# Score tile, exponentials and order of the value matmuls in a chunked-attention and routed-FFN kernel

## The chip, the cores and the metric

The kernel runs on one core of a Trainium2 chip. The metric is the device time of one execution in microseconds. A core has a matrix engine (TensorE, PE in the profile; its weight loads are the row PEld), a vector engine (VectorE, DVE), an activation engine (ScalarE, ACT), GpSimd (POOL), which here issues most DMAs, and a sync engine (SyncE, SP), which issues the others. PE writes to PSUM, eight banks of 128 partitions x 512 fp32.

## The reference

There are two steps. The first is attention over chunks, with 4 batches of 8 heads, 768 positions and 64 channels. Each chunk of 32 queries sees 8 memory keys and a window of the sequence around it:

```python
for c in range(nc):                       # chunk 32, left 16, right 8
    l_start, r_end = max(0, c * 32 - 16), min(S, c * 32 + 32 + 8)
    k_full = np.concatenate([mem_k, k[:, :, l_start:r_end]], axis=2)
    v_full = np.concatenate([mem_v, v[:, :, l_start:r_end]], axis=2)
    scores = np.matmul(q_c, k_full.transpose(0, 1, 3, 2)) / np.sqrt(D)
    a = softmax(scores)
    out[:, :, c * 32:c * 32 + 32] = np.matmul(a, v_full)
```

The second takes the result as x (4 batches, 768 rows, 512 columns). Per batch it scores each row by `x @ w_gate`, chooses the 128 highest, and adds `sigmoid(score) * relu(xe @ w1) @ w2` to those rows (w1 is 512 x 1024, w2 is 1024 x 512).

## The kernel before, in words

The unit of the attention is a pair of heads; there are 16 pairs (n = 0 to 15), four to a batch. The order on every engine is the order of the program text, written out by hand.

For each pair the stages are these. `tr_q` (L213) transposes q by 16 PE matmuls into PSUM, and ACT copies the result to `qT` (L219). `tr_k` (L227) does the same for k; DVE lays it out as overlapping windows in `kw` (L232), and POOL writes the memory keys into the gaps (L224). `tr_v` (L237) does v, with ACT's copy to `vw` (L242), and `back_v` (L245) transposes the windows back, with DVE's copy to `vc` (L251). `scores(n, half)` (L256) makes 8 matmuls into a PSUM tile of two banks, and ACT makes three exponentials of it (L271), one per mask column, each of 256 elements a partition. `values(n, half)` (L277) makes 12 matmuls into one bank: six of 96 output partitions and six of 32, which go to partitions 96 to 127. In the text all of the 96s come first, then all of the 32s (L288 to L293). DVE takes the reciprocal of the sums (L295) and writes x (L296). The transposes have 64 output columns of the array, the scores 64 rows, `back_v` the whole array.

PSUM is full: four banks for two score tiles (pool `pss`), one for the values (`pxx`), one for q's and `back_v`'s transposes (`pvv`), one for k's and v's (`ptt`), one for the second step (`pmm`).

The loop (L539 to L575) works on three pairs at once. In pass n it makes the first half of the scores of pair n+1, `tr_q(n+2)`, the first half of the values of pair n, `tr_k(n+2)`, the second half of the scores of n+1, `back_v(n+1)`, the second half of the values of n, and `tr_v(n+2)`. Between the stages stand eight hooks; hook 8n+j holds steps of the second step of the batch before, by a table of places (L477 to L483). `fill` matmuls of zeros (L114) stand where PE would do little.

The second step for a batch is: dots of x with w_gate on DVE (`m_dot`, L335), the scores as a row (`m_row`), comparisons of all with all on DVE (`m_cmp`, L373), counts by PE (`m_count`, L383), mask, slot and a one-hot matrix `sel` on DVE (`m_slot`, L398; `m_sel`, L405), the row numbers by PE and DVE (`m_aux`, L438 and L441), the fetch of the rows from DRAM by an indirect DMA of POOL (`m_fetch`, L412), their transposes (`m_rows`, L419), two FFN stages with ACT between them (L453, L455, L462, L465), and an indirect DMA that adds y to the output (L466). Batch 2 has its slot, sel and fetch at place 24, which is the start of pair 15; its FFN stands in the tail (L578 to L602). Batch 3 is done in the tail. It works in the banks of the score tiles and gathers its rows by PE from an f16 copy of x (`m_x16`, L340) instead of a DMA.

Weights and inputs come by POOL's DMAs, and SP stores x for batches 0 to 2 (L319, L320), POOL for batch 3.

Of the kernel before, what the change touches and what calls it, by code (L numbers as in the profile page):

```python
# [8 lines left out]
FP = mybir.dt.float32  # L9
# [17 lines left out]
def kernel(  # L27
# [13 lines left out]
    nc = tc.nc  # L41
# [72 lines left out]
    def fill_into(ap, n=1):  # L114
        for _ in range(n):
            nc.tensor.matmul(out=ap, lhsT=zeros[:, 0:128], rhs=zeros, start=True, stop=True)  # L116
# [138 lines left out]

    def scores(n, half, fills=0):  # L256
        if n >= NPR:
            return
        kw, qT = kws[n % SLOTS], qTs[n]
        qf = qT.rearrange("p t j -> p (t j)")  # L260
        p_s = pss.tile([128, 2, 512], FP, tag="ps", name="p_s")
        fill_into(p_s[:, 0, :], fills)
        for gi, g in enumerate(GROUPS[half]):
            for h in range(2):
                o = 64 * h
                nc.tensor.matmul(out=p_s[:, h, 96 * gi:96 * gi + 96], lhsT=kw[o:o + 64, g, :],  # L266
                                 rhs=qf[o:o + 64, 96 * g:96 * g + 96], start=True, stop=True)
        es = att.tile([128, 2, 4, 96], F16, tag="es", name="es")
        pv = p_s[:, :, 0:384].rearrange("p s (g t) -> p s g t", t=96)
        for c in range(3):  # L270
            nc.scalar.activation(out=es[:, :, :, 32 * c:32 * c + 32], in_=pv[:, :, :, 32 * c:32 * c + 32],  # L271
                                 func=AF.Exp, bias=maskb[:, c:c + 1], scale=0.125)
        ess[n, half] = es

    xs = {}

    def values(n, half, fills=0):  # L277
        b, pr = divmod(n, NP)
        if pr == 0 and half == 0:
            xs[b] = xpool.tile([128, NB, Dm], FP, tag="x", name=f"x{b}")  # L280
        es, vc = ess.pop((n, half)), vcs[n % SLOTS]
        if n == NPR - 1:
            p_w = pss.tile([128, 2, 512], FP, tag="ps", name="p_w")[:, 0, :]
        else:
            p_w = pxx.tile([128, 512], FP, tag="px", name="p_w")
        fill_into(p_w, fills)
        p_x = p_w[:, 0:390].rearrange("p (i h c) -> p i h c", i=3, h=2)
        for r0, r1, gis in ((0, 96, (0, 1, 2)), (96, 128, (3, 3, 3))):  # L288
            for i, gi in enumerate(gis):
                q0, q1 = (0, 96) if gi < 3 else (32 * i, 32 * i + 32)  # L290
                for h in range(2):
                    nc.tensor.matmul(out=p_x[r0:r1, i, h, :], lhsT=es[:, h, gi, q0:q1],  # L292
                                     rhs=vc[:, GROUPS[half][gi], h, 0:65], start=True, stop=True)  # L293
        rd = att.tile([128, 3, 2, 1], FP, tag="rd", name="rd")
        nc.vector.reciprocal(out=rd, in_=p_x[:, :, :, 64:65])  # L295
        nc.vector.tensor_tensor(  # L296
            out=xs[b].rearrange("p g (n h d) -> p n g h d", n=NP, d=D)[:, pr, 3 * half:3 * half + 3],
            in0=p_x[:, :, :, 0:64], in1=rd.to_broadcast([128, 3, 2, D]), op=ALU.mult)
# [7 lines left out]
    LAST = B - 1  # L306

    def m_bank(b, shape, dt=FP):

        if b == LAST:  # L310
            t = pss.tile([128, 2, 512], FP, tag="ps", name="p_l")
            return t
        return pmm.tile([128, 1, 512], FP, tag="pm", name="p_m")
# [155 lines left out]
    def moe_steps(b):  # L469
# [53 lines left out]
    fill(3)  # L523
    scores(0, 0)
    mem_rows(memv16, memvT)
# [4 lines left out]
    tr_k(1)  # L530
    scores(0, 1)
    fill(2)
# [3 lines left out]
    late_constants()  # L536
    scrA = mod.tile([128, NB], FP, tag="scrA", name="scrA")
    scrB = mod.tile([128, NB], FP, tag="scrB", name="scrB")
    for n in range(NPR):  # L539
# [98 lines left out]
```

## Time and profile before

| what | value |
|---|---|
| median of 3 runs | 139.21 us (139.1 to 145.28) |
| the profiled execution | 139.08 us, span of its profile 137.4 us |
| busy: PE, PEld | 111.7 us (81%), 83.0 us (60%) |
| busy: DVE, ACT, POOL | 87.5 us (64%), 80.0 us (58%), 50.5 us (37%) |
| mean granted PE clock | 0.936 of full |
| values matmuls L292 | 384, busy 24.4 us |
| exponentials L271 | 96, mean 485 ns, busy 38.8 us |
| end of the loop (last x of pair 15) | 111.9 us into the span |

The chain that ended last is spread over the engines: PE 31%, DVE 15%, ACT 14%, issue 14%, DMA 14%, POOL 6%. The granted clock was half of full from 61.7 to 68.5 us, from 106 to 112.8 us and at the very end. In the timeline a line gives the start and the length in us, the engine, the source line, the operation with its tiles, `128*96` for the rows and columns of the array that a matmul uses, and in brackets how long the engine stood idle before it and what ended that. A run of equal instructions is one line with its count; matmuls are pipelined, so the length of such a line goes past the start of the next.

### The profile page before, as it was taken

The numbers are of one execution on the slowest core, as the hardware profiler recorded it, in microseconds if no ns is written. First come the engines' busy times: TensorE is split into PE (matmuls) and PEld (weight loads), VectorE is DVE, ScalarE is ACT, GpSimd is POOL, SyncE is SP. The second block draws the span as 40 slices with busy tenths as digits, with TensorE's granted clock in tenths as the row PEclk, the third lists the DMA queues.
The fourth block names the chain that finished last, engine by engine and source line by source line (L and its number), as shares of the span: only waits on it lengthen the run. The fifth ranks groups of instructions, "written<-read, shape, count | busy, mean of one in ns | idle before, by whom it ended". The sixth has DMA issues, their size and how long they took to land.

```text
span 137.4 us, 4727 instructions
## 1 busy us (share of the span) xinstructions
PE 111.7 (81%) x2024; PEld 83.0 (60%) x2024; DVE 87.5 (64%) x280; ACT 80.0 (58%) x159; POOL 50.5 (37%) x84
## 2 busy tenths in 40 slices
PE   6997688977998978989997999897797897888500
PEld 2355376866777756867885858685656555458100
DVE  3444556574799399889738955997954896651000
ACT  4047958779779859565676947858748005153300
POOL 6996364352683634914200226121004140040130
PEclk9999999999999999995599999999999559999995
DMA  2999999999999999999991002973001439606050
GB/s 63 173 146 184 203 206 206 205 212 206 205 248 287 278 208 206 205 235 290 286 185 23 0 7 19 268 252 43 0 5 12 67 38 260 203 0 81 0 70 6
DMA packets 15397, 19.90 MB, mean 145 GB/s; under 512 B 848, under 2 KB 11536, under 8 KB 15376
## 3 DMA queue, kind: packets, MB, share of 16 engines
q0 software_dynamic: 12832, 14.62, 63.4%
q1 hardware_dynamic: 2544, 4.98, 11.0%
q8 instruction: 16, 0.26, 0.7%
q14 instruction: 5, 0.04, 0.1%
HBM read 24.25 MB, written 7.34 MB: 230 GB/s over the span
## 4 chain that ended last, share of the span: by engine, by line
PE 31%; DVE 15%; ACT 14%; issue 14%; DMA 14%; POOL 6%; POOLq 1%
ACT es L271 7%; DMA q<-in_q_dram 7%; PE p_w L292 7%; PE p_t L210 5%; PE p_v L250 4%; DMA xe<-out_dram,idx 3%; DMA out_dram<-y,idx 3%; DVE junk L335 3%; DVE x L296 3%; ACT qT L219 3%; PE p_w L116 3%; PE p_m L462 3%; PE p_m L453 2%; DVE gr L373 2%; PE p_m L383 2%
## 5 line engine op out<-in xcount | busy, mean ns | idle before, releaser
L271 ACT ACTIVATE es<-p_s,maskb 128x256 f16<-128x256 f32 x96 | 38.8, 485 | 3.2 <-PE p_s L266 3.1
L292 PEld LDWEIGHTS <-es 128*32 128x32 f16 (+1 forms) x384 | 22.1, 116 | 4.4 <-issue 0.7
L292 PE MATMUL p_w<-vc,es 128*32 128x65 f16 (+1 forms) x384 | 24.4, 208 | 0.0
L242 ACT COPY vw<-p_t 128x960 f16<-128x960 f16 x16 | 15.4, 962 | 14.5 <-PE p_t L210 14.5
L224 POOL COPY kw<-memkT 128x64 f16<-128x64 f16 x12 | 8.0, 666 | 36.4 <-DVE kw L232 36.4
L296 DVE TENSOR_TENSOR x<-p_w,rd 128x384 f32<-128x384 f32 x32 | 17.8, 558 | 1.1
L219 ACT COPY qT<-p_q 128x768 f16<-128x768 f16 x16 | 13.0, 813 | 7.4 <-PE p_q L210 7.4
L335 DVE SCALAR_TENSOR_TENSOR junk<-x,wgb 128x512 f32<-128x512 f32 (+1 forms) x30 | 16.2, 582 | 0.0
L466 POOL DMA_INDIRECT out_dram<-y,idx x4 | 6.5, 1635 | 24.7 <-ACT y L465 23.4
L295 DVE RECIPROCAL rd<-p_w 128x6 f32<-128x6 f32 x32 | 6.1, 191 | 12.5 <-PE p_w L292 12.1
L373 DVE TENSOR_SCALAR gr<-brow,scr 128x768 f16<-128x768 f32 x24 | 14.0, 623 | 0.1
L116 PE MATMUL p_f<-zeros 128*128 128x512 f16 x36 | 12.8, 496 | 1.3 <-DVE zeros L110 1.3
L250 PE MATMUL p_v<-ident,vw 128*128 128x128 f16 x128 | 10.2, 225 | 4.3 <-ACT qT L219 4.3
L251 DVE COPY vc<-p_v 128x1024 f16<-128x1024 f16 x16 | 11.0, 687 | 4.3 <-PE p_v L250 4.1
L232 DVE COPY kw<-p_t 128x1024 f16<-128x1024 f16 x16 | 10.9, 683 | 3.5 <-PE p_t L210 3.4
L266 PE MATMUL p_s<-qT,kw 64*128 64x96 f16 x256 | 11.3, 209 | 0.3 <-POOL kw L224 0.3
L250 PEld LDWEIGHTS <-vw 128*128 128x128 f16 x128 | 8.1, 100 | 5.6 <-issue 4.1
L116 PEld LDWEIGHTS <-zeros 128*128 128x128 f16 x60 | 5.9, 110 | 8.9 <-issue 4.6
L210 PE MATMUL p_q<-ident,q 96*64 96x96 f16 x256 | 8.8, 213 | 2.6 <-DMA q<-in_q_dram 2.5
L116 PE MATMUL p_w<-zeros 128*128 128x512 f16 x24 | 9.8, 410 | 1.0 <-DVE x L296 1.0
L210 PEld LDWEIGHTS <-q 96*64 96x64 f16 x256 | 6.7, 113 | 4.5 <-DMA q<-in_q_dram 2.7
L453 PEld LDWEIGHTS <-w_sb 128*128 128x128 f16 x128 | 7.6, 97 | 2.5 <-issue 1.6
(112 smaller groups left out, 165.0 us busy)
## 6 DMA issues: line engine op xcount, KB each, us to landing
out_dram<-x SPq DMA_DIRECT2D x3, 1152.0 KB, 11.5
k<-in_k_dram POOLq DMA_DIRECT2D x7, 384.0 KB, 13.2
q<-in_q_dram POOLq DMA_DIRECT2D x7, 384.0 KB, 13.7
v<-in_v_dram POOLq DMA_DIRECT2D x7, 384.0 KB, 14.6
w_sb<-in_moe_w_dram POOLq DMA_DIRECT2D x8, 256.0 KB, 13.4
out_dram<-x SPq DMA_DIRECT2D x3, 384.0 KB, 13.2
out_dram<-x POOLq DMA_DIRECT2D x1, 1152.0 KB, 6.8
k<-in_k_dram POOLq DMA_DIRECT2D x2, 192.0 KB, 4.8
```

Source lines behind the costliest of these rows:

```text
L116: nc.tensor.matmul(out=ap, lhsT=zeros[:, 0:128], rhs=zeros, start=True, stop=True)
L210: nc.tensor.transpose(out=dst[64 * h:64 * h + 64, j, :], in_=src[n][:, h, 64 * j:64 * j + 64], identity=ident16[0:96, 0:96])
L219: nc.scalar.copy(out=qT, in_=p_q.rearrange("p j t -> p t j"))
L242: nc.scalar.copy(out=vw.rearrange("p g (j t) -> p g j t", t=16)[:, :, :, 0:15], in_=_sap(p_t, 0, [[12, NG], [100, 8], [1, 15]]))
L250: nc.tensor.transpose(out=p_v[:, g, :, :], in_=vws[n % SLOTS][:, g, :], identity=ident16)
L251: nc.vector.tensor_copy(out=vcs[n % SLOTS][:, :, :, 0:64], in_=p_v)
L266: nc.tensor.matmul(out=p_s[:, h, 96 * gi:96 * gi + 96], lhsT=kw[o:o + 64, g, :], rhs=qf[o:o + 64, 96 * g:96 * g + 96], start=True, stop=True)
L271: nc.scalar.activation(out=es[:, :, :, 32 * c:32 * c + 32], in_=pv[:, :, :, 32 * c:32 * c + 32], func=AF.Exp, bias=maskb[:, c:c + 1], scal ...
L292: nc.tensor.matmul(out=p_x[r0:r1, i, h, :], lhsT=es[:, h, gi, q0:q1], rhs=vc[:, GROUPS[half][gi], h, 0:65], start=True, stop=True)
L296: nc.vector.tensor_tensor(out=xs[b].rearrange("p g (n h d) -> p n g h d", n=NP, d=D)[:, pr, 3 * half:3 * half + 3], in0=p_x[:, :, :, 0:64] ...
L335: nc.vector.scalar_tensor_tensor(out=junk[:, c0:c1], in0=x[:, bl, c0:c1], scalar=1.0, in1=wgb[:, c0:c1], op0=ALU.mult, op1=ALU.mult, accum ...
L373: nc.vector.tensor_scalar(out=m.gr[:, bl, :], in0=m.brow, scalar1=m.scr[:, bl:bl + 1], scalar2=None, op0=ALU.is_lt)
```

## The change

`scores(n)` makes all 16 matmuls of a pair into one tile of four banks, and there is one such tile in place of two smaller ones. Three exponentials of 512 elements a partition take the place of six of 256. In the loop `tr_q(n+2)` comes first and the whole of `scores(n+1)` after hook 8n; the second place of the scores is gone. `values` issues the 96 and the 32 output partitions by turns in place of one kind after the other. In pair 15 and the tail the banks of one four-bank tile are taken in turn (`last_bank`). The f16 copy of the first half of x of batch 3 moves ahead within pair 14. The dots of batch 3 are made whole in the tail, and no longer in two halves that are added. Batch 2's slot, sel and fetch move from place 24 to 30, which is behind the values of pair 15.

```diff
-    pss = ctx.enter_context(tc.tile_pool(name="pss", bufs=2, space=bass.MemoryType.PSUM))
+    pss = ctx.enter_context(tc.tile_pool(name="pss", bufs=1, space=bass.MemoryType.PSUM))
...
-    def scores(n, half, fills=0):
+    def scores(n):
...
-        p_s = pss.tile([128, 2, 512], FP, tag="ps", name="p_s")
-        fill_into(p_s[:, 0, :], fills)
-        for gi, g in enumerate(GROUPS[half]):
-            for h in range(2):
-                o = 64 * h
-                nc.tensor.matmul(out=p_s[:, h, 96 * gi:96 * gi + 96], lhsT=kw[o:o + 64, g, :],
-                                 rhs=qf[o:o + 64, 96 * g:96 * g + 96], start=True, stop=True)
-        es = att.tile([128, 2, 4, 96], F16, tag="es", name="es")
-        pv = p_s[:, :, 0:384].rearrange("p s (g t) -> p s g t", t=96)
+        p_s = pss.tile([128, 2, 2, 512], FP, tag="ps", name="p_s")
+        for half in range(2):
+            for gi, g in enumerate(GROUPS[half]):
+                for h in range(2):
+                    o = 64 * h
+                    nc.tensor.matmul(out=p_s[:, half, h, 96 * gi:96 * gi + 96], lhsT=kw[o:o + 64, g, :],
+                                     rhs=qf[o:o + 64, 96 * g:96 * g + 96], start=True, stop=True)
+        es = att.tile([128, 2, 2, 4, 96], F16, tag="es", name="es")
+        pv = p_s[:, :, :, 0:384].rearrange("p a s (g t) -> p (a s) g t", t=96)
+        ev = es.rearrange("p a s g t -> p (a s) g t")
         for c in range(3):
-            nc.scalar.activation(out=es[:, :, :, 32 * c:32 * c + 32], in_=pv[:, :, :, 32 * c:32 * c + 32],
+            nc.scalar.activation(out=ev[:, :, :, 32 * c:32 * c + 32], in_=pv[:, :, :, 32 * c:32 * c + 32],
                                  func=AF.Exp, bias=maskb[:, c:c + 1], scale=0.125)
...
         if n == NPR - 1:
-            p_w = pss.tile([128, 2, 512], FP, tag="ps", name="p_w")[:, 0, :]
+            p_w = last_bank()
...
-        for r0, r1, gis in ((0, 96, (0, 1, 2)), (96, 128, (3, 3, 3))):
-            for i, gi in enumerate(gis):
-                q0, q1 = (0, 96) if gi < 3 else (32 * i, 32 * i + 32)
-                for h in range(2):
-                    nc.tensor.matmul(out=p_x[r0:r1, i, h, :], lhsT=es[:, h, gi, q0:q1],
+
+        for i in range(3):
+            for h in range(2):
+                for r0, r1, gi, q0 in ((0, 96, i, 0), (96, 128, 3, 32 * i)):
+                    nc.tensor.matmul(out=p_x[r0:r1, i, h, :], lhsT=es[:, h, gi, q0:q0 + r1 - r0],
                                      rhs=vc[:, GROUPS[half][gi], h, 0:65], start=True, stop=True)
...
+    last = []
+
+    def last_bank():
+
+        if not last:
+            last.append(pss.tile([128, 4, 512], FP, tag="ps", name="p_l"))
+        last.append(None)
+        return last[0][:, len(last) % 4, :]
+
...
-                     counts=(21, 21, 21, 22, 22, 22), mask=22, slot=24, sel=24, fetch=24)
+                     counts=(21, 21, 21, 22, 22, 22), mask=22, slot=30, sel=30, fetch=30)
...
-        scores(n + 1, 0)
+        tr_q(n + 2)
         hook(i)
-        if n == NPR - 1:
-            m_dot(LAST, range(NB), 0, 2, scrA)
-        if 3 <= n + 3 < NPR:
+        if n + 3 < NPR:
             mem_cols(vws[(n + 3) % SLOTS], memvT, n + 3)
-        tr_q(n + 2)
+        scores(n + 1)
+        if n == NPR - 2:
+            m_x16(LAST, 0, NB, 0, 2)
         hook(i + 1)
         values(n, 0, nf)
         hook(i + 2)
         tr_k(n + 2)
         hook(i + 3)
-        scores(n + 1, 1)
-        if n == NPR - 2:
-            m_x16(LAST, 0, NB, 0, 2)
         hook(i + 4)
         back_v(n + 1)
...
-    m_dot(b, range(NB), 2, 4, scrB)
-    nc.vector.tensor_tensor(out=mods[b].scr, in0=scrA, in1=scrB, op=ALU.add)
+    m_dot(b, range(NB))
     fill(8)
```

More of the change, by code (lines that the diff above doesn't have):

```diff
@@ L260, in scores @@
         qf = qT.rearrange("p t j -> p (t j)")
-        p_s = pss.tile([128, 2, 512], FP, tag="ps", name="p_s")
-        fill_into(p_s[:, 0, :], fills)
-        for gi, g in enumerate(GROUPS[half]):
-            for h in range(2):
-                o = 64 * h
-                nc.tensor.matmul(out=p_s[:, h, 96 * gi:96 * gi + 96], lhsT=kw[o:o + 64, g, :],
-                                 rhs=qf[o:o + 64, 96 * g:96 * g + 96], start=True, stop=True)
-        es = att.tile([128, 2, 4, 96], F16, tag="es", name="es")
-        pv = p_s[:, :, 0:384].rearrange("p s (g t) -> p s g t", t=96)
+        p_s = pss.tile([128, 2, 2, 512], FP, tag="ps", name="p_s")
[8 more added lines that the diff above has]
+        ev = es.rearrange("p a s g t -> p (a s) g t")
         for c in range(3):
-            nc.scalar.activation(out=es[:, :, :, 32 * c:32 * c + 32], in_=pv[:, :, :, 32 * c:32 * c + 32],
+            nc.scalar.activation(out=ev[:, :, :, 32 * c:32 * c + 32], in_=pv[:, :, :, 32 * c:32 * c + 32],
                                  func=AF.Exp, bias=maskb[:, c:c + 1], scale=0.125)
-        ess[n, half] = es
+        ess[n] = es
     xs = {}
@@ L280, in values @@
             xs[b] = xpool.tile([128, NB, Dm], FP, tag="x", name=f"x{b}")
-        es, vc = ess.pop((n, half)), vcs[n % SLOTS]
+        es, vc = ess[n][:, half, :, :, :], vcs[n % SLOTS]
         if n == NPR - 1:
-            p_w = pss.tile([128, 2, 512], FP, tag="ps", name="p_w")[:, 0, :]
+            p_w = last_bank()
         else:
@@ L306 @@
     LAST = B - 1
+    last = []
[4 more added lines that the diff above has]
+        return last[0][:, len(last) % 4, :]
     def m_bank(b, shape, dt=FP):
         if b == LAST:
-            t = pss.tile([128, 2, 512], FP, tag="ps", name="p_l")
-            return t
+            return last_bank().unsqueeze(1)
         return pmm.tile([128, 1, 512], FP, tag="pm", name="p_m")
@@ L523 @@
     fill(3)
-    scores(0, 0)
+    scores(0)
     mem_rows(memv16, memvT)
@@ L530 @@
     tr_k(1)
-    scores(0, 1)
     fill(2)
@@ L536 @@
     late_constants()
-    scrA = mod.tile([128, NB], FP, tag="scrA", name="scrA")
-    scrB = mod.tile([128, NB], FP, tag="scrB", name="scrB")
     for n in range(NPR):
```

## The prediction

> **What bounds the kernel now.** I read the page's chain first: no engine holds more than a third of it (PE 31%), so each stage has a limit of its own and the question is who waits for whom inside one pair. Then the timeline of a quiet pair of batch 0 (no MoE work beside it), columns start, length, engine, line:
>
> ```profile
> 26.13 0.53 PE L210 MATMUL p_q<-ident,q 96*64 96x96 f16 x16
> 26.59 0.74 PE L292 MATMUL p_w<-vc,es 128*96 128x65 f16 x12
> 26.82 1.21 ACT L271 ACTIVATE es<-p_s,maskb 128x256 f16<-128x256 f32 x3
> 27.27 0.53 PE L210 MATMUL p_t<-ident,k 96*64 96x96 f16 x16
> 27.73 0.34 PE L266 MATMUL p_s<-qT,kw 64*128 64x96 f16 x8
> 27.90 0.82 ACT L219 COPY qT<-p_q 128x768 f16<-128x768 f16 x1
> 28.77 0.61 PE L250 MATMUL p_v<-ident,vw 128*128 128x128 f16 x8 [0.70 <-ACT qT L219]
> 29.21 0.38 PE L116 MATMUL p_w<-zeros 128*128 128x512 f16 x1
> 29.43 0.71 PE L292 MATMUL p_w<-vc,es 128*96 128x65 f16 x12
> 30.07 0.53 PE L210 MATMUL p_t<-ident,v 96*64 96x96 f16 x16
> 30.53 0.34 PE L266 MATMUL p_s<-qT,kw 64*128 64x96 f16 x8
> 30.80 0.53 PE L210 MATMUL p_q<-ident,q 96*64 96x96 f16 x16
> ```
>
> A pair takes 30.80 - 26.13 = 4.67 us. PE has one wait in it, 0.70 for ACT's qT. From start to next start PE's own work is tr_q 0.46, values 0.68, tr_k 0.46, scores 0.27, back_v 0.44, fill 0.22, values 0.64, tr_v 0.46, scores 0.27: 3.90 us. So ACT sets the pair, and PE follows 0.7 us behind. Where a row changes its array shape there is a gap, and three narrow windows of the same timeline show it inside one values set (the last 96-column matmul, the first 32-column one, the last 32-column one and what follows):
>
> ```profile
> 26.84 0.38 PE L292 MATMUL p_w<-vc,es 128*96 128x65 f16 x3
> ```
> ```profile
> 26.98 0.36 PE L292 MATMUL p_w<-vc,es 128*32 128x65 f16 x6
> ```
> ```profile
> 27.14 0.19 PE L292 MATMUL p_w<-vc,es 128*32 128x65 f16 x1
> 27.27 0.23 PE L210 MATMUL p_t<-ident,k 96*64 96x96 f16 x2
> ```
>
> Six 96-column matmuls start between 26.59 and 26.84 (0.05 apart). The next, of 32 columns, starts 0.14 after. Six of those follow to 27.14 (0.033 apart), and leaving that shape costs 0.13 again. A set of twelve pays for one change inside it and one behind it.
>
> Then the table of windows, for the later batches and the granted clock (columns: window, length, busy us of PE, PEld, DVE, ACT, POOL, then clock):
>
> ```profile
> 36.20:104.00 67.80, 60.58 (x1199) 48.23 (x1198) 53.18 (x151) 48.06 (x103) 21.45 (x33) 0.95 0.75 159
> ```
> ```profile
> 62.00:67.00 5.00, 5.00 (x84) 3.96 (x84) 4.10 (x13) 2.75 (x5) 1.56 (x2) 0.50 1.13 291
> ```
>
> From pair 4 to pair 14 PE is busy 60.6 of 67.8 us; DVE and ACT have 15 to 20 us to spare. PE is already nearly the bound there. The second line shows PE at half clock, in a stretch where it was never idle. Last the end, from the choice of batch 2's rows to their first use:
>
> ```profile
> 108.23 0.16 DVE L441 TENSOR_SCALAR idx<-p_m 128x1 int32<-128x1 f32 x1 [0.28 <-PE p_m L438]
> 109.31 1.04 POOL L412 DMA_INDIRECT xe<-out_dram,idx  x1 [3.85 <-DVE junk L335]
> 111.36 0.56 DVE L296 TENSOR_TENSOR x<-p_w,rd 128x384 f32<-128x384 f32 x1
> 113.61 0.39 PE L419 MATMUL p_e<-ident,xe 128*128 128x128 f16 x4
> ```
>
> **The change, part by part.** The sum is made against the profiled execution, 139.08 us (span 137.4); the median of the runs shown is 139.21, so the two agree within 0.2.
>
> *The order inside a values set.* The new loops issue a 96-column and a 32-column matmul by turns. That is 6 changes of 0.14 and 5 of 0.13 (taken at 0.125, the 27.14 row unrounded), 1.47 us to the last start and 0.13 behind it: 1.59 us, against 0.68 and 0.64 now. Price: 0.92 us a set. Bounds: if the two shapes ran side by side as the two 64-column halves of a transpose do (16 of them in 0.46 us, so a pair in 0.06), a set would take about 0.36 and gain 0.3; the upper end is 1.2 at half clock, where the same changes take 0.20 and 0.18. I take 0.92, since the row is the same change between the same two shapes in the same bank.
>
> The Trainium skill, "TensorEngine Tiling (Array Packing)", Key Properties, speaks both ways: tiles operate independently and may load and multiply in parallel, but changing the mode drains TensorE. By the first the sum would end near 130, by the second it stands as below.
>
> *Pairs 0 to 3.* PE's pair becomes 3.90 + 2 x 0.92, less 0.10 because sixteen score matmuls in one run save one change of shape (0.27 + 4 x 0.042 = 0.44 in place of 0.54): 5.64 us, over ACT's 3.3, so ACT's 0.70 wait is swallowed. 4 x (5.64 - 4.67) = 3.9. In pair 0 the first score half, which now precedes the wait for q's load, moves behind it: 0.3. Together +4.2.
>
> *Pairs 4 to 14.* 22 sets x 0.92 = 20.2, less 11 x 0.10. PE's waits in the window add to 6.7: on qT 2.2, on DVE's x 1.0, on kw 0.5 (these 3.7 vanish, as their producers get more time), on sel 1.2, brow 0.8, xeT and hT 1.0 (these 3.0 stay: each is a step just ahead of its user). 20.2 - 1.1 - 3.7 = +15.4; bounds 12.4 and 19.1.
>
> *Three wide exponentials.* Today each 256-element exponential takes 0.36 of ACT (26.82 to 27.90 for three). The nearest row of 512 elements with a per-partition operand is y:
>
> ```profile
> 82.09 0.69 ACT L465 ACTIVATE y<-p_m,gate 128x512 f32<-128x512 f32 x1 [1.98 <-PE p_m L462]
> ...
> 82.67 0.83 ACT L271 ACTIVATE es<-p_s,maskb 128x256 f16<-128x256 f32 x2
> ```
>
> It takes 0.58. Three cost 1.74 in place of 2.16, 0.42 a pair, 6.7 us in all. In the old schedule this would be worth up to 0.7 a pair; behind a PE of 5.64 it is worth 0. Its lower bound is no saving (a price by the run of 32 elements), also 0.
>
> *One score tile in place of two.* Scores of pair n+1 wait for the last exponential of pair n, with values, tr_k, back_v and tr_v queued behind them on PE. ACT's order becomes qT 0.68, three wide 1.74, vw 0.86: 3.3 us of a 5.64 us pair, so those exponentials end some 2 us before the next scores. Price 0; if ACT were late, up to 0.4 a pair. The tail's four-bank tile waits for the exponentials of pair 15, done in pair 14: 0.
>
> *x16 earlier in pair 14* (1.49 on ACT) now stands ahead of y: y, and POOL's scatter behind it, up to 1.5 late. The scatter precedes only the fetch, which is later still: 0.
>
> *Rows of batch 2 later, whole dots in the tail.* In pair 15 the values no longer wait for slot, sel and aux: PE ended its counts at 105.54 and began the values' fill at 108.06, so -2.5. Two slower sets: +2.0 (between 0.92 and 1.2 each). From the end of the second set (110.99) to p_e it is 2.6 now. After the change: x 0.93, slot 0.25, sel 1.1, aux and idx 0.5, then POOL's fetch, landing after 4.1 (109.31 to p_e, at most) to 4.8 (the fetch of batch 1): 7.4, so +4.9. The dots (6 x 0.61 = 3.7 on DVE instead of 12 x 0.345 with half of them earlier) end 6.5 behind the set, under that fetch; if it came early they would cap the gain at 0.9. On POOL the two stores of batch 3 stand behind the fetch, 2.8 later; only the last scatter needs them, 12 us on. SP's queue does not change. Together +4.4; bounds 2 and 6.
>
> *The clock.* I count a pair's array work as columns times the share of the 128*128 array in use: 48 transposes of 96 x 0.375, 16 scores of 96 x 0.5, 8 of 128, 24 values of 65 x 0.75 or 0.25, a fill of 512, together 4812. That was 1030 a us in batch 0 (4812 in 4.67), which never half-clocked; in 57.32 to 61.43, ahead of the half clock, 3481 in 4.11, 850. After the change batch 0 has 4812 in 5.64, 850; later pairs with a second fill 900, pair 7 with its one-column counts 740. I take two more stretches of 6.8 us than now. At half clock transposes take 0.78 and a set 2.26, a pair 9.3 in place of 5.9, so one costs 2.5: +5.0; bounds -2.5 (the old one goes) and +17.5 (seven more).
>
> The skill's "TensorE: Matmul & The Clock Gate", Part 1, has the gate close after an idle window of about 3.4 us. PE's longest wait in 57 to 62 was 0.39, so the trace does not agree. By that page the loop keeps its full clock and this term is 0.
>
> Sum: 139.1 + 4.2 + 15.4 + 4.4 = 163 without the clock, and + 5.0 = 168.
>
> **The rivals.** (1) *The shapes run side by side, and it is faster.* A set falls to 0.36, PE's pair to 3.2, and ACT's saving counts: batch 0 nears 3.5 a pair (-4.7), the middle meets DVE's 53.2 busy plus stalls (-6), the tail keeps +1.8: 130. For it: the transposes' halves. Against it: 0.14 at every 96-to-32 row. It decides by the cost of a set: between -0.3 (130) and +0.92 (163) the line crosses 139 near +0.05 us, so anything dearer than that is a loss. (2) *More is covered and the clock is no worse*: the 3.0 of short waits vanish too, tail +2, clock 0: 139.1 + 4.2 + 12.4 + 2 = 158. For it: every producer gets 20% more time. (3) *Half clock in much of the loop*: seven stretches, 163 + 17.5 = 181. For it: 850 a us in every pair of batch 0. Against it: one run's rows set that line. (4) *Scores wait for exponentials*: 15 x 0.4 more, 174; against it the 2 us of room.
>
> **How the numbers follow.** Forecast 0.50 (168, own range 161 to 175), rival 1 0.08, rival 2 0.17, rival 3 0.20, rival 4 0.05. The range 153 to 184 leaves out rival 1 and the far ends of 2 and 3, some 0.17. Within 2% (136.4 to 141.9, about what a measurement of this kernel can tell from no change) lies only a set that costs between -0.05 and 0.15: 0.03. Faster 0.08, slower 0.89.
>
> **What would show it.** A values set of 1.5 to 1.6 us from its first matmul to the next row at full clock; a pair of batch 0 at 5.6 with no PE wait on qT; wide exponentials of 0.7 each, 1.74 for three; p_e some 7.4 behind the last values set; more than one half-clock stretch before the tail. I am wrong if the 96- and 32-column starts lie closer than 0.1, if PE waits for es, or if the clock holds full throughout.

## The result, and the profile after

The changed kernel takes 207.44 us (median of four runs, 202.57 to 212.05), the kernel before 139.69 beside it: 1.46 times the time, with an interval from 1.436 to 1.485. It is slower, as forecast, but it lies 23 us beyond the upper end of the range. The profiled execution took 202.57 us, with a span of 199.8 and a mean granted clock of 0.669 (before: 137.4 and 0.936). Runs of one program differ as the clocks that they are granted do (0.617 to 0.669 in the four of the changed kernel), so every ratio here and below compares the undisturbed runs of two kernels on one chip, while a time is the median of all runs; the trace used here is of the run of 202.57.

The page of the changed kernel (span; busy us, share and count of each engine; PE's busy tenths and the clock's tenths in 40 slices of 5 us; the chain; the two groups that the change touches):

```profile
span 199.8 us, 4662 instructions
PE 179.2 (90%) x2024; PEld 124.9 (62%) x2024; DVE 87.9 (44%) x267; ACT 73.0 (37%) x111; POOL 49.8 (25%) x84
...
PE   7979999999999999999999999999989968788530
...
PEclk9978999655555555555555599555559955559985
...
PE 70%; issue 10%; DMA 8%; POOL 4%; DVE 3%; POOLq 1%; ACT 1%; DVEq 0%
...
L293 PE MATMUL p_w<-vc,es 128*96 128x65 f16 x360 | 65.2, 245 | 0.0
...
L272 ACT ACTIVATE es<-p_s,maskb 128x512 f16<-128x512 f32 x48 | 29.7, 696 | 0.3 <-PE p_s L266 0.2
```

PE's share of the chain goes from 31% to 70%, and PE hardly rests in the loop, yet the clock row (tenths of the full clock) stands at 5 for most of the loop. DVE and POOL do the same work as before. ACT's 48 wide exponentials take 29.7 us where 96 took 38.8.

A quiet pair of batch 0 in the timeline of the changed kernel (PE's rows alone; start, length, engine, line, operation), which answers to the pair shown of before:

```profile
24.06 1.84 PE L293 MATMUL p_w<-vc,es 128*96 128x65 f16 x12
25.83 0.53 PE L210 MATMUL p_t<-ident,k 96*64 96x96 f16 x16
26.29 0.62 PE L250 MATMUL p_v<-ident,vw 128*128 128x128 f16 x8
26.78 0.39 PE L116 MATMUL p_w<-zeros 128*128 128x512 f16 x1
27.01 1.80 PE L293 MATMUL p_w<-vc,es 128*96 128x65 f16 x12
28.74 0.53 PE L210 MATMUL p_t<-ident,v 96*64 96x96 f16 x16
29.10 0.51 PE L210 MATMUL p_q<-ident,q 96*64 96x96 f16 x16
29.54 0.51 PE L266 MATMUL p_s<-qT,kw 64*128 64x96 f16 x16
29.98 1.84 PE L293 MATMUL p_w<-vc,es 128*96 128x65 f16 x12
```

A set of twelve now runs from 24.06 to 25.83 and from 27.01 to 28.74: 1.77 and 1.73 us, with the change of shape behind it (0.68 and 0.64 before). No PE row has a bracket: the 0.70 wait on qT is gone, and none on `es` has come. The pair takes 29.98 - 24.06 = 5.92. ACT's three exponentials in it run from 24.93 for 1.86 us.

The table of windows of the changed kernel (window, length, busy us and count of PE, PEld, DVE, ACT, POOL, then clock, DMA share, GB/s): this pair, the first half-clock stretch, one whole pair in it, and the stretch after it:

```profile
24.06:29.98 5.92, 5.92 (x101) 4.51 (x97) 2.92 (x7) 3.40 (x6) 1.82 (x3) 1.00 1.24 207
36.60:115.10 78.50, 78.20 (x826) 56.48 (x828) 38.52 (x102) 29.73 (x47) 18.05 (x30) 0.50 0.57 112
42.60:51.80 9.20, 9.20 (x106) 6.57 (x102) 4.02 (x11) 3.41 (x5) 2.53 (x4) 0.50 1.13 243
...
115.10:125.40 10.30, 10.30 (x184) 7.79 (x186) 3.85 (x10) 5.28 (x9) 2.94 (x3) 1.00 0.14 19
```

The clock fell at 36.6, in the last pair of batch 0, and stayed at half for 78.5 us in which PE was busy for 78.2. A pair takes 9.2 there. Two more such stretches follow (125.4 to 149.3, 159.5 to 180.0), and the span ends in a fourth. Before, the half-clock stretches were 6.8 us each.

**The sum, redone.** The last values set ended 110.99 us into the span before and 163.12 after, so 52.1 of the 62.4 us lie ahead of that point and 10.3 behind it. In the loop ahead of it the clock is at half for 78.5 + 23.9 + 3.6 = 106 us, against 6.8 + 4.9 = 11.7 before. A pair that takes 9.2 at half clock and 5.92 at full loses 1 - 5.92/9.2 = 0.36 of its time, so the 94 extra us cost about 34. (The pair of 9.2 has one fill more than that of 5.92. By pairs 6 and 7, which e14 below runs at full clock with the same work, the share is 0.34 and the cost 32.) What is left, 18 to 20, is the alternation at full clock less what it covers. Behind that point, p_e (the transposes of batch 2's fetched rows, the first step of its FFN) comes 6.45 us after the set (2.6 before, +3.8), and from p_e to the end it takes 30.2 (23.8 before, +6.4).

### The profile page after: what moved, and what is told of

Read it like the earlier page. It is cut to its first block, busy times and chain, and to the rows that moved or that the text cites. A ratio compares the mean times of both kernels' runs of the same rounds, so it can differ in the third digit from the quotient of the medians.

```text
span 199.8 us, 4662 instructions
## 1 busy us (share of the span) xinstructions
PE 179.2 (90%) x2024; PEld 124.9 (62%) x2024; DVE 87.9 (44%) x267; ACT 73.0 (37%) x111; POOL 49.8 (25%) x84
## 4 chain that ended last, share of the span: by engine, by line
PE 70%; issue 10%; DMA 8%; POOL 4%; DVE 3%; POOLq 1%; ACT 1%; DVEq 0%
PE p_w L293 30%; PE p_t L210 9%; PE p_v L250 5%; PE p_s L266 5%; PE p_w L116 5%; DMA q<-in_q_dram 5%; PE p_q L210 4%; PE p_m L461 3%; PE p_m L354 2%; DMA out_dram<-y,idx 2%; PE p_l L293 2%; PE p_m L470 2%; PE p_m L391 2%; PE p_m L446 1%; DVE x L297 1%
## 5 line engine op out<-in xcount | busy, mean ns | idle before, releaser
L293 PE MATMUL p_w<-vc,es 128*96 128x65 f16 x360 | 65.2, 245 | 0.0
L293 PEld LDWEIGHTS <-es 128*96 128x96 f16 (+1 forms) x384 | 46.8, 122 | 28.8 <-issue 9.7
L242 ACT COPY vw<-p_t 128x960 f16<-128x960 f16 x16 | 15.4, 962 | 57.4 <-DVE x L297 36.2
L272 ACT ACTIVATE es<-p_s,maskb 128x512 f16<-128x512 f32 x48 | 29.7, 696 | 0.3 <-PE p_s L266 0.2
L343 DVE SCALAR_TENSOR_TENSOR junk<-x,wgb 128x512 f32<-128x512 f32 x24 | 15.5, 684 | 0.0
L116 PE MATMUL p_f<-zeros 128*128 128x512 f16 x36 | 13.9, 533 | 1.3 <-DVE zeros L110 1.3
L250 PE MATMUL p_v<-ident,vw 128*128 128x128 f16 x128 | 14.5, 283 | 0.0
L461 PEld LDWEIGHTS <-w_sb 128*128 128x128 f16 x128 | 11.0, 126 | 3.4 <-issue 3.1
L250 PEld LDWEIGHTS <-vw 128*128 128x128 f16 x128 | 11.2, 128 | 2.3 <-issue 0.6
L116 PE MATMUL p_w<-zeros 128*128 128x512 f16 x22 | 12.4, 564 | 0.0
L210 PE MATMUL p_t<-ident,k 96*64 96x96 f16 x256 | 12.0, 259 | 0.0
L210 PE MATMUL p_t<-ident,v 96*64 96x96 f16 x256 | 11.8, 256 | 0.0
## 6 DMA issues: line engine op xcount, KB each, us to landing
out_dram<-x SPq DMA_DIRECT2D x3, 1152.0 KB, 10.4
```

Of the source, the lines that this page charges most:

```text
L210: nc.tensor.transpose(out=dst[64 * h:64 * h + 64, j, :], in_=src[n][:, h, 64 * j:64 * j + 64], identity=ident16[0:96, 0:96])
L242: nc.scalar.copy(out=vw.rearrange("p g (j t) -> p g j t", t=16)[:, :, :, 0:15], in_=_sap(p_t, 0, [[12, NG], [100, 8], [1, 15]]))
L250: nc.tensor.transpose(out=p_v[:, g, :, :], in_=vws[n % SLOTS][:, g, :], identity=ident16)
L272: nc.scalar.activation(out=ev[:, :, :, 32 * c:32 * c + 32], in_=pv[:, :, :, 32 * c:32 * c + 32], func=AF.Exp, bias=maskb[:, c:c + 1], scal ...
L343: nc.vector.scalar_tensor_tensor(out=junk[:, c0:c1], in0=x[:, bl, c0:c1], scalar=1.0, in1=wgb[:, c0:c1], op0=ALU.mult, op1=ALU.mult, accum ...
L461: nc.tensor.matmul(out=p_h[:, 0, 128 * fi:128 * fi + 128], lhsT=w1_sb[:, dch, f0:f0 + 128], rhs=m.xeT[:, dch, :], start=(dch == 0), stop=( ...
```

## The experiments

Four theories were told apart. A: each change between the 96- and the 32-wide shape costs TensorE time, and the thinner array work then lowers the granted clock, which costs more than the change itself. Its rivals: the loss comes from the wide score tile and the order of the loop (B in the texts on record); it comes from going back and forth between places of the array, whatever the shape (C in the texts on record); or the late rows of batch 2 and the tail hold it. "Rows later" and "FFN later" below are places in the table of hooks. The kernel before was timed again on every chip, with medians of 140.45 (e1, e2, e3, e5), 141.72 (e4, e7, e8, e9), 144.01 (e10 to e13) and 140.7 (e14, e15).

**The alternation taken out of the changed kernel** (e1_after_grouped): all 96s first, then all 32s.

```diff
-        for i in range(3):
-            for h in range(2):
-                for r0, r1, gi, q0 in ((0, 96, i, 0), (96, 128, 3, 32 * i)):
+        for r0, r1, gis in ((0, 96, (0, 1, 2)), (96, 128, (3, 3, 3))):
+            for i, gi in enumerate(gis):
+                q0, q1 = (0, 96) if gi < 3 else (32 * i, 32 * i + 32)
+                for h in range(2):
```

> The changed kernel with one part undone: a values set again issues its six 96-column matmuls first and its six 32-column ones behind them. Theory A (the alternation is the cause, by its changes of shape and by the clock that falls with them): a set back at 0.68 at full clock, no half-clock stretch longer than 7 us in the loop, and a time of 132 to 144 us. Theory B (the single score tile, the wide exponentials or the new order of the loop are the cause, the alternation only shows it): still above 165 us, with PE waiting on es or p_s.

149.8 us (148.03 to 153.98): of the loss of 68 us about 9 are left (149.8 against 140.45). Its pair of batch 0, PE's rows in the timeline:

```profile
22.62 0.51 PE L266 MATMUL p_s<-qT,kw 64*128 64x96 f16 x16
23.07 0.74 PE L294 MATMUL p_w<-vc,es 128*96 128x65 f16 x12
...
26.60 0.51 PE L266 MATMUL p_s<-qT,kw 64*128 64x96 f16 x16
```

It takes 3.98 us where before takes 4.67: the rest of the change does what it says in a quiet pair, and PE has 3.93 of it busy. The 9 us are lost elsewhere. The time came out above the 132 to 144 expected: taking the alternation out leaves a kernel that is still slower than before, which e7 to e13 look into.

**The alternation alone in the kernel before** (e2_before_alternated): the same edit the other way round.

```diff
+        for i in range(3):
+            for h in range(2):
+                for r0, r1, gi, q0 in ((0, 96, i, 0), (96, 128, 3, 32 * i)):
```

> The kernel before with one part of the change alone: the 96- and 32-column matmuls of a values set by turns, two score tiles and everything else as before. Theory A: the whole loss, 190 to 215 us, mean clock below 0.72, one half-clock stretch of more than 30 us. Theory B: within 10 us of the kernel before, or at most 168 us, which is what the changes of shape cost at full clock.

193.11 us (191.21 to 204.77), ratio 1.378 (1.352 to 1.403). The order of one loop does most of the damage by itself, 0.38 of the 0.46 that is lost. The clock row of its page:

```profile
PEclk9999555555555555555555555995555797579995
```

It falls at 20.2 us, in batch 0, and holds at half for 105.8 us, with pairs of 9.1. This trace is of the run of 204.77 us, with a mean clock of 0.642; the three shortest runs have 0.708 to 0.715.

**Two of a shape at a time** (e5_after_two_by_two): 96, 96, 32, 32 and so on, 5 changes inside a set in place of 11.

```diff
-            for h in range(2):
-                for r0, r1, gi, q0 in ((0, 96, i, 0), (96, 128, 3, 32 * i)):
+            for r0, r1, gi, q0 in ((0, 96, i, 0), (96, 128, 3, 32 * i)):
+                for h in range(2):
```

> The changed kernel with a values set in the order 96, 96, 32, 32 and so on: 5 changes of shape inside a set in place of 11. Theory A: at full clock a set takes 6 x 0.045 and 5 x 0.14 and one more behind it, about 1.1 us, half of the way from 0.66 to 1.76. If the clock holds, 145 to 152 us; if it falls in the same way, 165 to 185. Theory B: as the changed kernel, above 195.

165.05 us (158.04 to 183.82), between the two, with 4.6 us a pair of batch 0 and 1.08 to 1.11 a set: fewer changes, less loss. The wide spread goes with the clock of its runs, 0.858 down to 0.679: the same program takes 158 us at the one and 184 at the other.

**Going between places without a change of shape** (e4_after_columns_of_32): a 96-wide matmul becomes three of 32, so that a set is 24 matmuls of one shape that go round four places of the array.

```diff
-                for r0, r1, gi, q0 in ((0, 96, i, 0), (96, 128, 3, 32 * i)):
-                    nc.tensor.matmul(out=p_x[r0:r1, i, h, :], lhsT=es[:, h, gi, q0:q0 + r1 - r0],
+                for r in range(4):
+                    gi, q0 = (i, 32 * r) if r < 3 else (3, 32 * i)
+                    nc.tensor.matmul(out=p_x[32 * r:32 * r + 32, i, h, :], lhsT=es[:, h, gi, q0:q0 + 32],
```

> The changed kernel with every values set cut into 24 matmuls of 32 output columns by turns over the four column places of the array, so that all of a set has one shape: twice the matmuls, no change of shape inside a set. Theory A (it is the change of shape that costs, not the going back and forth between places): a set takes at most 24 x 0.033 = 0.8 and 0.13 behind it, and half of that if places run side by side; 135 to 152 us. Theory C (any alternation between places of the array costs): above 180 us.

152.41 us (150.79 to 157.96), ratio 1.079 (1.067 to 1.091). A set in its timeline, at full clock:

```profile
24.89 0.37 PE L294 MATMUL p_w<-vc,es 128*32 128x65 f16 x24
25.19 0.53 PE L210 MATMUL p_t<-ident,k 96*64 96x96 f16 x16
...
26.48 0.37 PE L294 MATMUL p_w<-vc,es 128*32 128x65 f16 x24
26.79 0.53 PE L210 MATMUL p_t<-ident,v 96*64 96x96 f16 x16
```

A set of 24 takes 0.30 us, less than half of the grouped set of twelve (0.64 to 0.68) and a sixth of the alternated one. Theory C falls: it is the change of shape that costs, and matmuls of one shape in different places do run side by side. Whether the gap at a change is the array running empty or a weight load that has to wait, these runs do not tell apart. This is also the set that rival 1 of the prediction wanted (0.36), and the kernel still takes 152 and not 130, so a cheaper set is no gain here (150.79 at the lowest, 148.03 with e1's grouped sets). In this trace, of the run of 153.8 us, the mean clock is 0.806, and one pair has 1.68 us of PE's idle time in the middle of k's transposes that no other engine or transfer accounts for.

**More array work** (e3_after_more_fills, and later e15_after_four_fills): the changed kernel with two, and with four, more `fill` matmuls of zeros ahead of every values set.

```diff
-        fill_into(p_w, fills)
+        fill_into(p_w, fills + 2)
```

> The changed kernel with two more matmuls of zeros of 512 columns ahead of every values set: 64 more, 0.216 us each at full clock, 13.8 us of added work on PE. Theory A with a clock that answers to the array's work: 4812 + 2048 columns in some 6.8 us of a pair of batch 0 are 1010 a us, as much as the kernel before had, so the clock holds, and more work makes it faster: 163 + 14, about 175 to 185 us, mean clock above 0.85. A clock that answers only to PE's idle time: the added work adds its own time at half clock, 215 to 230 us.

192.18 us (186.57 to 194.61). The page counts 2088 matmuls in place of 2024, so 64 fills of 0.22 us are added, some 14 us of work at full clock, and the kernel is 15 us faster than the changed one (186.57 to 194.61 against 202.57 to 212.05, on another chip). A pair of batch 0 in it, from the table of windows:

```profile
43.00:49.70 6.70, 6.70 (x109) 4.76 (x105) 2.68 (x6) 3.41 (x5) 2.07 (x4) 1.00 0.53 74
```

It takes 6.7 us at full clock at a time when the changed kernel takes 9.2; the clock stayed full from 31.1 to 85.8, and its mean is 0.865 (0.669 in the changed kernel). With four:

> The changed kernel with four more matmuls of zeros ahead of every values set (two more gave 187 to 195 us at a clock of 0.85 to 0.90). 128 more make 27.6 us of added work at full clock. If the clock is held by the array's work: mean clock 0.93 or more and 163 + 28 = 191, up to 200. If two fills already held it as far as fills can, 0.85 to 0.90 and 200 to 212.

204.29 us (202.59 to 208.09), ratio 1.461 (1.439 to 1.482), mean clock 0.906 to 0.915 (0.867 in the slowest run). In the trace the clock is full from 6.0 to 81.1, with 7.6 us a pair, but the fills now cost what they save. Both came out slower than theory A expected (by 7 and by 4 us at the near end); the time with four lies in the range of the other expectation, its clock between the two. The clock still falls where the rows of a batch are counted and chosen: here at 81.1, 125.5 and 169.9. So the clock answers to the work put into the array, but neither two nor four fills a set pay for the changes of shape.

**Is half clock a state that holds itself?** (e14_after_two_bursts): the changed kernel with a burst of 24 fills ahead of pairs 5 and 9, and nothing else.

```diff
+        if n in (5, 9):
+            fill(24)
         tr_q(n + 2)
         hook(i)
```

> The changed kernel with 24 matmuls of zeros at the head of pairs 5 and 9, 48 in all, 10.4 us of PE work at full clock and 20.5 at half. In the changed kernel the clock fell at 36.6 us and stayed at half for 78.5. If the half clock holds itself, because a pair of 9.2 us does too little a us to open it, a dense burst opens it within 7 us and the pairs behind the burst take 6 to 6.5 until it falls again: pairs 5 to 8 gain some 3 each, the time is near that of the changed kernel, 195 to 210, at a mean clock above 0.75. If the clock goes by something else, it stays at half through the burst: 220 to 230.

203.86 us (198.68 to 205.36), so the bursts cost about what they bring; the trace, of the run of 205.36 us, is what this run is for. Its windows: the whole half-clock stretch, the burst's part of it up to the opening, what follows, and one pair of that:

```profile
20.50:64.90 44.40, 44.30 (x452) 31.15 (x453) 17.73 (x42) 15.09 (x22) 10.07 (x19) 0.50 0.90 166
61.50:64.90 3.40, 3.40 (x9) 1.19 (x10) 1.76 (x6) 0.90 (x1) 0.00 (x0) 0.50 1.07 192
64.90:88.80 23.90, 23.90 (x356) 16.82 (x354) 12.79 (x30) 10.76 (x18) 8.76 (x14) 1.00 0.49 76
75.00:81.50 6.50, 6.50 (x110) 4.74 (x106) 4.36 (x13) 3.78 (x7) 2.23 (x4) 1.00 1.13 179
```

The burst begins at 61.5; 3.4 us later the clock opens, and pairs 6 and 7 take 6.5 and 6.1 us, where the changed kernel takes 9.8 and 9.2 for the same two. The clock falls again at 88.8, right behind the one-column counts (87.2 to 88.8); the second burst, from 99.6, is followed by another 30.7 us at full clock, from 102.5. So the loop runs at either clock with the same instructions, and a denser stretch is what brings it back up.

**The wide tile without the alternation** (e7_wide_tile_alone): the score tile, the wide exponentials and the loop's new order; values grouped, rows at 24, dots in halves, the first values of pair 15 in their old bank. The core of the edit against the changed kernel:

```diff
-        if n == NPR - 1:
+        if n == NPR - 1 and half == 1:
             p_w = last_bank()
...
-                     counts=(21, 21, 21, 22, 22, 22), mask=22, slot=30, sel=30, fetch=30)
+                     counts=(21, 21, 21, 22, 22, 22), mask=22, slot=24, sel=24, fetch=24)
```

> The one score tile, the three wide exponentials and the new order of the loop alone: a values set in the old order, rows of batch 2 at place 24, the dots of batch 3 in two halves, the first values of pair 15 in their old bank. The prediction's terms: batch 0 at 3.9 to 4.0 a pair in place of 4.67 (-2.8), later pairs up to 3.7 less, tail as before. 133 to 138 us if the clock is that of the kernel before; 140 to 146 if a shorter loop falls to half clock more often. Theory B (one score tile costs waits): slower, with PE waiting on es.

147.28 us (146.4 to 147.83), ratio 1.053 (1.043 to 1.062): neither of the two expected. It is ahead for two thirds of the loop: pair 10 ends at 72.4, before's at 76.5. Then its timeline has this, a load of v and the fetch of batch 0's rows on POOL, PE's wait for those rows, and one step in pair 14:

```profile
55.08 0.67 POOL L83 DMA_DIRECT2D v<-in_v_dram  x1 [0.31 <-PE p_m L392]
60.69 1.05 POOL L421 DMA_INDIRECT xe<-out_dram,idx  x1 [2.10 <-PE p_t L210]
...
74.64 0.61 PE L428 MATMUL p_e<-ident,xe 128*128 128x128 f16 x4 [3.68 <-DMA xe<-out_dram,idx]
...
106.70 0.71 ACT L474 ACTIVATE y<-p_m,gate 128x512 f32<-128x512 f32 x1
107.45 0.17 PE L389 MATMUL p_m<-zero,ltri 128*128 128x6 f16 x1 [0.99 <-ACT y L474]
```

The rows land 13.9 us after the issue of the fetch. Ahead of it in POOL's queue stand three loads of 384 KB issued from 53.41 to 55.08. The view of the transfers from 55 to 80 us has the last of them and the fetch, with the us from issue to landing at the end:

```profile
v<-in_v_dram POOLq DMA_DIRECT2D x1, 384.0 KB, 18.9
xe<-out_dram,idx POOLq DMA_INDIRECT x1, 13.9
```

So v lands at 74.0 and the rows at 74.6. When the fetch is issued hardly matters: ten traces, before among them, issue it between 60.7 and 68.0 us and have it land at 74.3 to 74.8 (e4, which issues the load of v at 62.1 where these ten have 55.1 to 59.2, at 77.3). No run took the loads away. Before, p_e of batch 0 stands at 75.1, here at 74.6. Pair 11 takes 12.6 us in place of 7.4, and the lead is gone. Then y, in pair 14, waits for the x16 that was moved ahead of it, and PE for y (0.99).

**The parts of those 8 us.** A fill in every set (e9_wide_tile_fills), in e7:

```diff
-        fill_into(p_w, fills)
+        fill_into(p_w, max(fills, 1))
```

> The one score tile, wide exponentials and new loop order alone, with a matmul of zeros ahead of every first values set (8 more, 1.7 us of PE work): it asks whether the clock, and not a wait, decides what this part is worth. If so: mean clock at 0.93 or more and 132 to 137 us, at or under the same kernel without them. If fills only add work: 1 to 2 us over it.

145.76 us (144.35 to 150.74), ratio 1.039 (1.027 to 1.051), clock 0.915 to 0.93 in three of its runs (0.864 to 0.919 in e7), and not the 132 to 137 expected: no slower for the added work, but the clock is not where most of the 8 us lie.

Two tail banks as two tiles (e10_wide_tile_two_tail_tiles), in e7:

```diff
-            last.append(pss.tile([128, 4, 512], FP, tag="ps", name="p_l"))
-        return last[0][:, len(last) % 4, :]
+        if len(last) % 2:
+            return pss.tile([128, 4, 512], FP, tag="ps", name="p_l")[:, 0, :]
+        return pvv.tile([128, 512], FP, tag="pv", name="p_k")
```

> The one score tile, wide exponentials and new loop order alone, with the tail's banks taken by turns from two tiles in place of the slices of one. If a PE write to one bank of the shared tile waits for the reader of another bank of it (in the tail of that kernel PE waits 0.7 on brow, on xeT and twice on hT, and 0.4 on gate), this takes 2 to 3 us off: 144 to 145. If those waits are the data's own: 147 as before.

143.76 us (142.57 to 144.02), ratio 1.027 (1.015 to 1.039) where e7 has 1.053: some 3.5 us, a little more than the 2 to 3 expected. The other way round, the kernel before with its two tail tiles as two halves of one (e13_before_one_tail_tile):

```diff
-            t = pss.tile([128, 2, 512], FP, tag="ps", name="p_l")
-            return t
+            if not last:
+                last.append(pss.tile([128, 2, 512], FP, tag="ps", name="p_l"))
+            last.append(None)
+            return last[0][:, len(last) % 2, :].unsqueeze(1)
```

> The kernel before with one part alone: in the tail the two banks taken by turns are slices of one tile in place of two tiles. If dependences go by tile: 2 to 3 us slower, 142 to 144. If they go by the bytes: as before.

144.86 us (143.13 to 150.57), ratio 1.026 (1.007 to 1.046). From p_e to the end it takes 26.9 in place of 23.8 us. PE's waits in its tail that name the shared tile (us in all, times, longest):

```profile
PE p_l L456 <- ACT hT L458: 0.7, 1, 0.7
PE p_l L441 <- ACT xeT L435: 0.7, 1, 0.7
...
PE p_l L465 <- ACT hT L458: 0.7, 1, 0.7
PE p_l L349 <- ACT brow L355: 0.7, 1, 0.7
...
PE p_l L456 <- DVE gate L446: 0.4, 1, 0.4
```

The work and the banks are the same as before; only the tile is one. Of these five waits, 3.2 us, before has none; it has one of 0.6 on xeT in their place. PE now waits until ACT or DVE has read the other bank, so dependences in this program go by tile, and what looks like four banks in turn is one buffer. The changed kernel has the same five waits, and one of 0.9 on DVE's x in pair 15.

Rows later in the kernel before (e8_before_rows_later):

```diff
-                     counts=(21, 21, 21, 22, 22, 22), mask=22, slot=24, sel=24, fetch=24)
+                     counts=(21, 21, 21, 22, 22, 22), mask=22, slot=30, sel=30, fetch=30)
```

> The kernel before with slot, sel and fetch of batch 2 at place 30, behind the last values, and nothing else. The prediction's term: -2.5 for values that wait for nothing, +4.9 from the last values set to p_e, so about 2 to 3 us slower at the same clock, 141 to 144; more, up to 150, if the idle PE lets the clock fall over the FFN of the tail. If the fetch is hidden anyway: 138 to 140.

142.91 us (140.9 to 146.2), ratio 1.008 (0.997 to 1.019): the same within 2%, and at the near end of the 141 to 144 expected.

FFN of batches 0 and 1 later, so that PE does not wait for their fetch (e11_wide_tile_ffn_later, in e7), and this with the two tail tiles and x16 back in its old place (e12_wide_tile_all_three; the first hunk is e11's whole edit):

```diff
-                 counts=(30, 30, 30, 31, 31, 31), mask=31, slot=34, sel=35, fetch=37, rows=54, ffn=(55, 57, 59))
+                 counts=(30, 30, 30, 31, 31, 31), mask=31, slot=34, sel=35, fetch=37, rows=57, ffn=(58, 60, 61))
...
-        if n == NPR - 2:
-            m_x16(LAST, 0, NB, 0, 2)
         hook(i + 1)
...
+        if n == NPR - 2:
+            m_x16(LAST, 0, NB, 0, 2)
         hook(i + 4)
```

> The one score tile, wide exponentials and new loop order alone, with the transposes and FFN of batch 0's rows three places later (57, 58, 60, 61 in place of 54, 55, 57, 59). The fetch of these rows lands at 74.6 us, behind the input loads in the same queue, whatever the loop has gained by then; PE waits 3.7 for it. If that is where the 4 us that pairs 0 to 10 gain are given back: the wait goes and 2 to 3 us with it, 144 to 145. If the loop only waits elsewhere: 147.

> The one score tile, wide exponentials and new loop order with the two mends above, and the f16 copy of x behind the third hook of pair 14 again, where y does not stand behind it. If the losses add up: 147 less 2.5, 2.5 and 1, about 139 to 142, level with the kernel before or a little under it; under 137 only if the clock holds as well.

e11 takes 151.8 us (146.03 to 154.88); PE's wait for the rows falls from 3.7 to 1.9, but its clock is 0.837 to 0.906 and pair 11 still takes 12.6 in the trace (of the run of 154.88 us), so it decides nothing. e12 takes 145.93 (143.73 to 147.53), ratio 1.033 (1.013 to 1.052): each wait named is gone or smaller, but the gains do not add up, and no version beat the kernel before.

## Why the prediction was wrong

It had the direction and the mechanism; one term of its sum, the half clock, was too small by a factor of more than six. By its own steps:

- **Order inside a values set: right, mis-sized a little.** 1.77 and 1.73 us for the 1.59 predicted, so about 1.1 a set for 0.92, shown by e1 and e2. A quiet pair took 5.92 for 5.64.
- **Pairs 0 to 14 and the cover: right.** The wait on qT went, and what is left of the loop's loss after the clock is taken out is 18 to 20 us, where the steps for the pairs and the two slower sets of pair 15 gave 4.2 + 15.4 - 2.5 + 2.0 = 19.1. That the two agree so closely is partly luck: the sets' extra 0.18 is some 5 us over 30 sets (an estimate), so about as much more than was counted on must have been covered.
- **Wide exponentials and the single score tile: right.** 0.696 us each, 1.86 for three (1.74 predicted), worth nothing behind a PE of 5.9; no wait on `es`, so rival 4 did not happen.
- **Rows of batch 2: nearly right.** p_e 6.45 behind the set for 7.4 predicted. By itself (e8, ratio 1.008 with 1 inside its interval) it cost some +1, for a net +2.4 at the sets' old price (-2.5 + 4.9).
- **"The tail's four-bank tile ...: 0": wrong.** 3 us (e10, e13), since its banks do not come free one by one. The remaining +3.3 behind p_e lies beside 10.4 us of half clock (169.6 to 180.0), which before had none of between p_e and its last microseconds; this was not tried apart.
- **x16 earlier: 0 was wrong, by little.** PE waits 0.3 for y in the changed kernel, and 0.99 where the sets are grouped (e7; 1.0 in e1 and e10). The step looked at POOL's scatter behind y and not at PE's counts, which take y's bank.
- **The step that failed: "I take two more stretches of 6.8 us than now ... one costs 2.5: +5.0; bounds -2.5 ... and +17.5 (seven more)".** Measured: 94 us more of half clock in the loop, at 0.34 to 0.36 each, about +32 to +34. The step had the right quantity, array work per us, and saw that batch 0 would stand at the line (850 predicted, 4812/5.92 = 813 measured). It then counted stretches of the length seen in the trace of before, as if each ended by itself; that was the mistake. At half clock the same pair, with a second fill 5324 columns, takes 9.2 us: 580 a us. A loop that thin did not open the clock again. What did is denser work: a fill does its 512 columns in some 0.42 us there, 1220 a us, and a run of those opened it after 3.4 us in e14; in the changed kernel it opened at 115.1, with FFN matmuls of 128 columns since 113.2. In before, the first stretch ended at 68.5, with `back_v` and the transposes of a score row from 67.3 on, the second at 112.9, with the eight fills of the tail from 110.9 on.

The clock records tell more. In all 16 traces the clock changes a whole number of steps of 3.41 us after the change before it: 6.8, 78.5, 10.3 and 23.9 us are 2, 23, 3 and 7 steps. Count the columns of each step as the prediction does, from the matmuls of the traces (727 steps). Of 142 steps under 600 columns a us one was followed by full clock; of 391 above 900, all but one, whichever clock the step itself ran at; between the two both occur, and a border of 790 sorts 693 of the 727 rightly. From 19.6 us on the steps of the changed kernel had 821, 837, 1008 and 825; the next, up to 36.6, had 696, and the clock fell. So the same loop lies over the border at full clock (813) and under it at half (580), and that is how half clock holds itself. This is read from the traces; no run was made for it, and the border is not sharp.

Rival 3 (181) named this, and its bound was seven stretches of the old length. The right bound was "the rest of the loop at the half-clock price": some 11 pairs x (9.3 - 5.9) = 37, which gives 200 with the prediction's own 163, and the range should have reached there.

The Trainium skill, "TensorE: Matmul & The Clock Gate", Part 1, lets the gate close after an idle window of about 3.4 us. The measurement decides against that as the only cause: by the profile PE was busy for 78.20 of the 78.50 us at half clock. The 3.4 us in which the burst of e14 opened the clock, and the steps of 3.41 us, agree with the window's length.

The skill's "TensorEngine Tiling (Array Packing)", Key Properties, was weighed from both sides in the prediction, and the traces agree with each half in its place: with tiles that work independently in e4 (24 matmuls in 0.30 us), and with a price at each change of mode in the changed kernel (11 changes make a set 1.77); that the price is a drain no run shows.

Rival 1 also had a wrong premise. Its 130 us was the price of a loop with cheap sets; e4 has sets of 0.30 and takes 152, e7 has grouped ones and takes 147. A quiet pair does fall to 4 us, but the lead ends at a fetch that lands at 74.6 (74.5 in before), however early the loop comes to it, and is spent.

What stays open: the exact rule by which the clock falls. Pairs of 1020 to 1050 columns a us kept it in before, and for a while in e3 and e5; 813 lost it at 36.6 us in the changed kernel, and e2 at 20.2. The 34 steps that the border of 790 sorts wrongly are not explained. More than half of e7's loss is not explained by the waits named either: with all three mended e12 is still at 1.033, where e7 has 1.053.

## What to carry to other kernels

Issue small matmuls grouped by their array shape, or cut them all to one shape; alternating two shapes paid a gap at each change, in all some 1.1 us a set. When a change thins out TensorE's work, count that work per us and, if it nears the rate at which the clock was seen to fall, price it at the lower clock for the whole loop that follows and not for the stretches seen so far, because at the lower clock the loop does still less work per us; ask which denser work would bring it back. And before a saving in a loop is counted, find the first transfer in the trace that lands at a time of its own: a lead is worth nothing past it.

## What the runs showed of the hardware that was not expected

- The clock changed only in steps of 3.41 us, and by the array work of the step before: half clock under 600 columns a us, full above 900, with one exception each in 142 and 391 steps.
- Half clock held itself for 78.5 us (after) and 105.8 us (e2) with PE busy throughout, and a burst of full-array matmuls opened it in 3.4 us.
- Adding some 14 us of matmuls of zeros to the changed kernel made it 15 us faster (e3).
- 24 matmuls of 32 output columns, going round four places, take 0.30 us; 12 in two shapes, grouped, 0.64 to 0.68; alternated, 1.73 to 1.77 (all at full clock, for the same result).
- Two halves of one PSUM tile, in two banks, waited for each other as one buffer: 3.1 us in a tail of 24 (e13). This is the program's own order of waits.
- An indirect fetch of 128 rows landed 13.9 us after its issue with loads ahead of it in the queue (e7), and 3.6 us after it in the tail of the changed kernel; issued anywhere from 60.7 to 68.0 us, it landed at 74.3 to 74.8 (ten traces).
